# Window attention and two feed-forward layers on one core: the written list of the first pass is laid out anew

## Chip, core and metric

The kernel runs on one core of a Trainium2 chip. The metric is the device time of one execution in microseconds (us). The core has a matrix engine (TensorE, PE in the profile; its weight loads are PEld), three elementwise engines (VectorE is DVE, ScalarE is ACT, GpSimd is POOL) and a queue that starts transfers (SyncE, SP). Each engine takes its instructions strictly in the order in which the program hands them over, and waits where an operand or a buffer is not ready.

## The reference

```python
k_sum = k.reshape(B, H, nb, block, D).max(axis=3)      # B,H,S,D = 2,8,768,64; block 32
v_sum = v.reshape(B, H, nb, block, D).mean(axis=3)
scores_l = where(|i - j| < 16, q @ k.T / sqrt(D), -1e9)
scores_s = q @ k_sum.T / sqrt(D) + log(block)
a = softmax(concat([scores_l, scores_s]))
x = (a @ concat([v, v_sum])).transpose(0, 2, 1, 3).reshape(1536, 512)
h = relu(x @ w_in1); x = (h * h) @ w_out1               # 512 -> 2048 -> 512
h = x @ w_in2; P = a0 + a1*h + a2*h^2 + a3*h^3
out = (P / (1 + |b0|*|h| + |b1|*h^2 + 1e-6)) @ w_out2
```

## The kernel before

Attention is cut into 12 **units** (256 tokens by 4 heads), each of two **duos**, 24 in all. The feed-forward layers keep each operand as a coarse part and a remainder (`wh`, `wl`, `xh`, `xl`, `sh`, `sl`) and make three matmuls for a product. They run in four passes over the weights. The first pass takes only the first 5 of the 16 column blocks of layer 1, token group after token group (four of 256 tokens, one of 512), so 25 steps, and it runs while attention is still under way. From there on a loop (`main_loop`) orders the work; until there the order is a list written out by hand, `ORDER`, of 783 items. A program walks through it and emits each item's instructions, so the list alone fixes what stands behind what on every engine. An item is a letter and a number; a `*` means that a copy is made by VectorE where it would otherwise be made by ScalarE or GpSimd.

- Transfers (SP): `E F` keys, `q_ Q` queries, `v Z` and `N` values, `J` keys of the second batch, `I` raw weights (three buffers).
- Keys and block sums: `P R` rearranging copies, `t` transposes on PE, `l k` copies out of PSUM, `c B` block maxima; `S` sums on GpSimd, `V` matmuls, `u w` copies.
- Attention of unit u: `q` transposes, `z` copy. Of duo d: `s` scores (PE, matrix `pss`; both duos of a unit must be done before either goes on), `m` mask and row maximum (VectorE, L505), `e` exponentials (ScalarE, L514), `r` row sum and reciprocal (VectorE, L522, L523), `n` normalising (GpSimd, L529), `p` transposes (PE, `ptp`), `b` copy (`pp`, ScalarE or VectorE), `o` the product with values (PE, `pav`). Then `x` coarse part (ScalarE) and `y` remainder (VectorE) of the unit's output.
- Weights, half a block each: `T` (ScalarE, L146), `D` (VectorE, L154 and L155), `W` (ScalarE, L166), `M` (GpSimd, L171). Tile `wdec` has two buffers, so `T` of n waits for `M` of n-2.
- First pass: `h` a quarter of a step of layer 1 (three matmuls, L612), `i` relu (ScalarE, L622), `j` square (VectorE, L627), `G` coarse part (ScalarE, L675), `H` remainder (GpSimd, L682), `Y` a quarter of a step of layer 2 (three matmuls, L706). Steps 0 to 3, 4 and so on are `h0` to `h3`, ...; the last five steps (`h80` to `h99`) take 512 tokens at once and need the last four units. `X` are filling matmuls with no use but to keep PE busy.

Six PSUM banks go round among `pk`, `pt`, `pss`, `ptp`, `pvs`, `pav`: a bank is reused in the order in which the list gives it back. The walk through the list:

```python
for x in ORDER.split():
    ...
    elif x[-1] == "*":
        parts[x[0]](int(x[1:-1]), dve)
    else:
        parts[x[0]](int(x[1:]))
main_loop()
```

Of the kernel before, what the change touches and what calls it, by code (L numbers as in the profile page):

```python
# [16 lines left out]


ORDER = (
    "E0 _i0 X8 _m0 _id _m1 F0 K0 P0 F1 E1 E2 q_0 F2 _bw I0 E3 q_1 R0* P1 F3 t0 X2 _ml R1 t1 l0 "  # L20
    "P2 k0 q0 _m2 l1 k1 R2 z0 v0 c0 P3 X3 t2 c1 v1 l2* R3 s0 s1 q1 Q1 S0 _pr k2 T0 I1 v3 B0 t3 "
    "c2 m0 B1 S1 D0 B2 e0 z1 m1 N0 l3* e1 r0 r1 n0 k3 V0 W0 p0 q2 v2 u0 c3 z2 n1 w0 s2 s3 m2 e2 "
    "r2 T1 b0* M0 m3 N1 n2 B3* D1 p1 I2 S2 s4 s5 m4 q3 p2 e3 S3 N2 N3 b1* e4 o0 o1 r3 I3 n3 V1 "
    "z3 m5 T2 x0 p3 r4 u1 W1 D2 w1 n4 M1 b2* W2 b3* e5 y0 h0 M2 o2 o3 x1 p4 s6 s7 m6 r5 T3 h1 I4 "
    "y1 h2 O0 h3 e6 T4 D3 i0 D4 n5 Q2 h4 h5 j0 W3 b4 h6 p5 q4 W4 M3 m7 q5 M4 h7 z4 i1 G0 I5 H0 "
    "h8 e7 r6 h9 I6 N4 Y0 b5* Y1 Y2 Y3 h10 j1 T5 r7 n6 N5 T6 z5 D5 h11 p6 J1 D6 o4 o5 n7 W5 i2 "
    "G1 J0 s8 s9 m8 M5 W6 b6* I7 p7 m9 x2 b7 M6 t4 e8 H1 j2 I8 y2 T7 T8 h12 h13 N6 h14 N7 l4* "
    "_b8 D7 Y4 D8 J2 h15 Y5 J3 Y6 Y7 i3 N9 W7 G2 W8 H2 o6 o7 M8 Y8 x3 Y9 Y10 Y11 M7 e9 j3 I9 h16 "
    "h17 r8 r9 h18 h19 k4 n8 y3 h20 i4 h21 j4 G3 H3 n9 T9 h22 N11 h23 Z0 h24 Y12 Y13 D9 Y14 J5 "
    "Y15 I10 h25 h26 i5 j5 h27 h28 N8 h29 p8 G4 W9 H4 M9 t5 i6 G5 Y16 Y17 H5 Y18 Y19 h30 Y20 j6 "  # L30
    "b8 I11 N10 Y21 Y22 h31 Y23 I12 i7 S4 p9 h32 G6 h33 l5 s10 s11 m10 e10 r10 n10 h34 j7 h35 "
    "b9* h36 Q3 Q4 H6 m11 e11 o8 o9 p10 Y24 r11 Y25 Y26 T10 D10 Y27 n11 i8 h37 T11 G7 b10* I13 "
    "h38 k5* j8 h39 p11 W10 x4 H7 i9 Y28 Y29 G8 D11 H8 Y30 Y31 Y32 y4 b11 W11 c4 Y33 Y34 J4 o10 "
    "o11 M10 V2 J6 J7 M11 x5 h40 h41 y5 T12 h42 h43 i10 j9 G9 Y35 t6 Z1 D12 W12 h44 H9 Y36 c5 "
    "T13 k6* q6 z6 j10 h45 D13 Y37 h46 M12 h47 Y38 i11 G10 H10 Y39 h48 B4 l6 Y40 Y41 Y42 I14 u2 "
    "N13 j11 Y43 B5* h49 h50 N15 h51 i12 h52 t7 W13 c6 G11 w2 h53 l7* h54 S5 H11 h55 k7 j12 s12 "
    "s13 m12 e12 r12 Y44 m13 Y45 n12 i13 G12 c7 T14 H12 I15 Y46 Y47 q7 e13 r13 p12 Y48 M13 Y49 "
    "Y50 q8 z7 b12 Y51 s14 s15 N12 n13 j13 z8 h56 D14 m14 h57 m15 p13 h58 e14 h59 b13 r14 B7 N14 "
    "i14 V3 I16 n14 G13 e15 o12 o13 u3* H13 Q5 w3* p14 T15 Y52 r15 Y53 Y54 Y55 x6 y6 W14 h60 b14 "
    "n15 p15 j14 q9 b15* h61 D15 B6 o14 o15 M14 x7 s16 s17 m16 e16 y7 h62 h63 h64 W15 M15 m17 "  # L40
    "h65 h66 z9 i15 G14 I17 H14 Y56 e17 Y57 Y58 j15 r16 h67 i16 G15 n16 r17 Y59 h68 T16 h69 h70 "
    "H15 h71 Y60 j16 i17 Y61 G16 I18 Y62 H16 N18 n17 Y63 T17 D16 j17 Y64 N17 Y65 Y66 h72 Y67 N16 "
    "W16 N19 h73 q10 D17 p16 s18 s19 m18 e18 r18 z10 I19 h74 M16 h75 m19 b16* h76 p17 n18 W17 "
    "e19 i18 G17 b17* o16 o17 M17 I20 H17 j18 r19 s20 s21 m20 N21 p18 x8 Y68 m21 e20 N20 Y69 Y70 "
    "n19 Y71 r20 e21 n20 h77 b18* y8 h78 q11 h79 z11 p20 r21 p19 s22 s23 m23 b19* n21 o18 o19 "
    "i19 m22 G18 e23 p21 H18 N22 Y72 r23 e22 b21* b20 r22 Y73 n23 x9 n22 T18 Y74 o20 o21 x10 y9 "
    "T19 p23 b23* y10 N23 Y75 p22 h80 b22 j19 o22 o23 h81 D18 I21 x11 W18 y11 h82 h83 i20 M18 "
    "D19 G19 h84 h85 H19 h86 j20 T20 Y76 Y77 W19 Y78 h87 Y79 h88 i21 M19 h89 j21 G20 h90 H20 h91 "
    "D20 Y80 i22 Y81 G21 Y82 I22 H21 Y83 T21 D21 Y84 W20 Y85 M20 Y86 Y87 T22 h92 h93 j22 h94 W21 "
    "h95 i23 I23 h96 h97 M21 G22 h98 H22 D22 h99 Y88 j23 Y89 Y90 W22 Y91 i24 G23 j24 H23 M22 T23 "  # L50
    "D23 W23 M23 "
)


# [854 lines left out]
```

## Time and profile before

| | |
|---|---|
| time before, median of 3 runs | 633.11 us (631.19 to 633.25) |
| the profiled execution's own time | 633.35 us |
| its span, first to last instruction | 631.6 us |
| PE busy over the span | 601.4 us (95%) |
| DVE, ACT, POOL busy | 380.6, 389.6, 347.8 us (60%, 62%, 55%) |
| mean clock granted to PE | 0.981 |

The profiled execution is 0.24 us above the median. Nearly 2 us lie outside the span. In the second half of the span PE stands at nine tenths or more in every slice, so read the first ten of the 40 slices of the page for anything that another order of the list can touch.

### The profile page before, as it was taken

How to read it: one execution, taken by the hardware profiler on the slowest of the kernel's cores; microseconds unless marked ns; L12 is line 12 of the kernel's file. 1: busy time of each engine (PE TensorE's matmuls, PEld its weight loads, DVE VectorE, ACT ScalarE, POOL GpSimd, SP SyncE). 2: the span in 40 equal slices, each digit the busy share in tenths (PEclk: the TensorE clock that was granted, in tenths of full speed). 3: DMA queues.
4: the chain of work that ended last, by engine and by line, in shares of the span. 5: the costliest groups of instructions: out<-in, count | busy, mean ns of one | idle time of the engine just before them, and what ended most of it. 6: DMA issues, size and time to landing. Idle time of an engine off the chain costs nothing.

```text
span 631.6 us, 9882 instructions
## 1 busy us (share of the span) xinstructions
PE 601.4 (95%) x3578; PEld 506.5 (80%) x3578; DVE 380.6 (60%) x791; ACT 389.6 (62%) x715; POOL 347.8 (55%) x363
## 2 busy tenths in 40 slices
PE   6678999888999999999999999999999999999997
PEld 6568887777888888888888888888888888888885
DVE  5776387757644333111146477898787887676775
ACT  5566456745544444222156678989888988777772
POOL 3667767553464444422277658776655774444442
PEclk8788999989999999999999999999999999999999
DMA  9949967421333323000024410221201300010011
GB/s 219 240 130 216 231 158 179 118 79 42 116 108 100 100 81 97 1 0 1 0 68 168 134 33 34 67 67 35 66 34 33 101 1 1 1 66 1 10 58 66
DMA packets 65376, 51.49 MB, mean 82 GB/s; under 512 B 39856, under 2 KB 59056, under 8 KB 65328
## 3 DMA queue, kind: packets, MB, share of 16 engines
q1 hardware_dynamic: 65184, 50.74, 29.4%
q8 instruction: 28, 0.46, 0.3%
q14 instruction: 20, 0.16, 0.1%
q10 hardware_dynamic: 144, 0.13, 0.1%
HBM read 47.71 MB, written 3.15 MB: 81 GB/s over the span
## 4 chain that ended last, share of the span: by engine, by line
PE 86%; DVE 5%; POOL 2%; DMA 2%; ACT 2%; issue 1%; SPq 0%; DVEq 0%; POOLq 0%; ACTq 0%
PE h L612 40%; PE y L706 40%; DMA early<-in_k_dram 2%; PE pav L559 2%; PE pss L489 2%; DVE pr L505 1%; ACT pr L514 1%; POOL pr L529 1%; PE ptp L539 1%; DVE mx L522 1%; DVE pp L543 1%; POOL sl L682 1%; PE pk L402 1%; PE pvs L441 1%; PE pt L467 0%
## 5 line engine op out<-in xcount | busy, mean ns | idle before, releaser
L612 PE MATMUL h<-xl,wh 128*128 128x512 f32 (+1 forms) x424 | 157.5, 371 | 5.0 <-DVE xl L581 3.7
L612 PE MATMUL h<-xh,wh 128*128 128x512 f32 (+1 forms) x424 | 158.7, 374 | 2.0 <-DVE r L627 2.0
L612 PE MATMUL h<-xh,wl 128*128 128x512 f32 (+1 forms) x424 | 156.9, 370 | 0.7 <-POOL wl L171 0.7
L682 POOL TENSOR_TENSOR sl<-r,sh 128x512 fp32r<-128x512 f32 (+1 forms) x58 | 65.5, 1129 | 105.8 <-PE y L706 76.0
L636 POOL TENSOR_TENSOR q<-q,u 128x512 f32<-128x512 f32 x48 | 65.2, 1359 | 96.1 <-ACT q L633 94.2
L627 DVE TENSOR_TENSOR r<-r,h 128x512 f32<-128x512 f32 (+1 forms) x58 | 34.3, 592 | 117.0 <-ACT r L622 107.3
L612 PEld LDWEIGHTS h<-xl,wh 128*128 128x128 f32 x424 | 80.3, 189 | 19.5 <-DVE xl L581 6.3
L612 PEld LDWEIGHTS h<-xh,wh 128*128 128x128 f32 x424 | 80.3, 189 | 16.6 <-DVE r L627 2.2
L171 POOL TENSOR_TENSOR wl<-wdec,wh 128x512 fp32r<-128x512 f32 x64 | 83.4, 1309 | 17.4 <-ACT wh L166 13.0
L612 PEld LDWEIGHTS h<-xh,wl 128*128 128x128 f32 x424 | 80.2, 189 | 14.2 <-POOL wl L171 0.9
L706 PE MATMUL y<-sl,wh 128*128 128x512 f32 (+1 forms) x232 | 82.7, 357 | 1.3 <-POOL sl L682 0.8
L706 PE MATMUL y<-sh,wh 128*128 128x512 f32 (+1 forms) x232 | 83.0, 358 | 0.0
L706 PE MATMUL y<-sh,wl 128*128 128x512 f32 (+1 forms) x232 | 82.0, 353 | 0.0
L622 ACT ACTIVATE r<-h 128x512 f32<-128x512 f32 (+1 forms) x58 | 30.3, 522 | 81.3 <-PE h L612 43.1
L706 PE MATMUL y<-wh,sl 128*128 128x512 f32 x192 | 74.9, 390 | 0.1
L706 PE MATMUL y<-wh,sh 128*128 128x512 f32 x192 | 74.7, 389 | 0.0
L706 PE MATMUL y<-wl,sh 128*128 128x512 f32 x192 | 74.7, 389 | 0.0
L682 POOL TENSOR_TENSOR sl<-p,sh 128x512 fp32r<-128x512 f32 x48 | 63.1, 1316 | 8.5 <-ACT sh L675 7.2
L658 DVE SCALAR_TENSOR_TENSOR q<-q,h 128x512 f32<-128x512 f32 x48 | 32.9, 686 | 41.6 <-ACT h L654 41.6
L529 POOL TENSOR_SCALAR pr<-pr,rs 128x120 f32<-128x120 f32 x96 | 38.8, 425 | 31.1 <-DVE rs L523 20.4
L706 PEld LDWEIGHTS y<-sl,wh 128*128 128x128 f32 x232 | 44.0, 190 | 8.8 <-POOL sl L682 2.8
L166 ACT CAST wh<-wdec 128x512 fp32r<-128x512 f32 x64 | 39.7, 620 | 18.1 <-DVE wdec L155 17.1
(92 smaller groups left out, 1055.6 us busy)
## 6 DMA issues: line engine op xcount, KB each, us to landing
wraw<-in_moe_w_in_dram SPq DMA_DIRECT2D x32, 512.0 KB, 3.9
wraw<-in_moe_w_out_dram SPq DMA_DIRECT2D x32, 512.0 KB, 3.3
early<-in_v_dram SPq DMA_DIRECT2D x40, 96.0 KB, 4.8
out_dram<-acc SPq DMA_DIRECT2D x11, 256.0 KB, 2.1
acc<-in_q_dram SPq DMA_DIRECT2D x10, 256.0 KB, 5.8
early<-in_k_dram SPq DMA_DIRECT2D x8, 192.0 KB, 4.8
early<-in_v_dram SPq DMA_DIRECT2D x4, 384.0 KB, 7.2
kst<-in_k_dram SPq DMA_DIRECT2D x8, 192.0 KB, 4.2
```

Source lines behind the costliest of these rows:

```text
L166: nc.scalar.copy(out=wt[n][0][:, j], in_=f32(wdec[n, j]))
L171: nc.gpsimd.tensor_tensor(out=tl[:, j], in0=t, in1=f32(th[:, j]), op=ALU.subtract)
L489: nc.tensor.matmul(psc[u][e][w * LO:(w + 1) * LO, c * HK:(c + 1) * HK], lhsT=qz[u % 2][r, c * P + w * LO:c * P + (w + 1) * LO], rhs=kt[2 * ...
L529: nc.gpsimd.tensor_scalar(out=pr[:, c, 0:HK], in0=pr[:, c, 0:HK], scalar1=rs[:, c:c + 1], scalar2=1.0, op0=ALU.mult, op1=ALU.mult,)
L559: nc.tensor.matmul(pav[u][e * D:(e + 1) * D, c * P + w * LO:c * P + (w + 1) * LO], lhsT=vn[u % 2][j][:, w, f:f + D], rhs=po[2 * u + e][:, ...
L612: nc.tensor.matmul(hq[g][:, 0:n], lhsT=w[:, 0, ws], rhs=x[:, part, ts], start=(part == 0 and j == 0), stop=(part == KC - 1 and j == 2),)
L622: nc.scalar.activation(out=r, in_=hq[g][:, 0:n], func=AF.Relu)
L627: nc.vector.tensor_tensor(out=eq[g], in0=eq[g], in1=hq.pop(g)[:, 0:n], op=ALU.mult)
L636: nc.gpsimd.tensor_tensor(out=q_, in0=q_, in1=u_, op=ALU.mult)
L658: nc.vector.scalar_tensor_tensor(out=q_, in0=q_, scalar=1.0 + 1e-6, in1=z_, op0=ALU.add, op1=ALU.mult)
L682: nc.gpsimd.tensor_tensor(out=sl[:, 0:n], in0=eq.pop(g), in1=f32(sh[:, 0:n]), op=ALU.subtract)
L706: nc.tensor.matmul(o, lhsT=lt, rhs=rt, start=(f == 0 and j == 0 and d * m % 512 == 0), stop=(f == FS[ps] - 1 and j == 2 and (d + 1) * m % ...
```

## The change

Only the string `ORDER` differs. It has the same 783 items, but the 783 stand in another order, and 24 copies have another engine. From ScalarE or GpSimd to VectorE go `P0 k0 R1 R2 w1 k7 b12 u2 w2 b14 b20 b22`, from VectorE to ScalarE or GpSimd `R0 l2 b1 b2 b5 b6 l4 l7 B5 b16 b21 b23`. Nothing is computed otherwise. Two stretches of the table, around `s18`:

```diff
-    "W16 N19 h73 q10 D17 p16 s18 s19 m18 e18 r18 z10 I19 h74 M16 h75 m19 b16* h76 p17 n18 W17 "
-    "e19 i18 G17 b17* o16 o17 M17 I20 H17 j18 r19 s20 s21 m20 N21 p18 x8 Y68 m21 e20 N20 Y69 Y70 "
...
+    "q11 G12 H12 Y46 Y47 s18 s19 W11 z11 m18 r17 N15 o14 e18 o15 h56 h57 h58 Y48 G13 h59 Y49 N17 "
+    "p16 m19 Y50 Y51 i14 N16 n17 r18 b16 p17 H13 h60 s20 s21 b17* o16 x7 o17 N19 n18 M11 h61 y7 "
+    "h62 j14 h63 h64 h65 e19 m20 r19 n19 e20 G14 H14 r20 n20 p18 b18* x8 N18 Y52 Y53 Y54 Y55 p19 "
```

ScalarE near the start, from the second and third block sums (`early<-pvs`) to the first coarse output of attention (`xh<-pav`), of before:

```order
L474 COPY qz_86<-pt 128x512
L146 ACTIVATE wdec<-wraw 128x512
L576 CAST xh<-pav 128x2x256
L449 COPY early<-pvs 24x256 x2
L166 CAST wh<-wdec 128x512
```

and of the change:

```order
L448 COPY early<-pvs 24x256 x4
L542 COPY pp_89<-ptp 120x512
L448 COPY early<-pvs 24x256 x2
L513 ACTIVATE pr_102<-pr_102,mx_90 128x120 x4
L473 COPY qz_85<-pt 128x512
L145 ACTIVATE wdec<-wraw 128x512
L473 COPY qz_86<-pt 128x512
L575 CAST xh<-pav 128x2x256
```

The first output now stands behind the block sums of both units, one more group of exponentials and both copies of queries of units 4 and 5; PE makes the scores of duos 6 and 7 and the transposes of 3, 4 and 5 ahead of the first product.

PE around the transposes of duo 17 (`ptp<-ident,pr_104`), of before (the names behind `pav` are the copies of duos 16 and 17):

```order
L612 MATMUL h<-xl,wh 128x256
L612 MATMUL h<-xh,wl 128x256
L539 MATMUL ptp<-ident,pr_104 120x128 x4
L559 MATMUL pav<-pp_88,early 64x64
L559 MATMUL pav<-pp_89,early 64x64
```

and of the change:

```order
L705 MATMUL y_1580<-sl,wh 128x256
L538 MATMUL ptp<-ident,pr_104 120x128 x4
L611 MATMUL h<-xh,wh 128x256
L611 MATMUL h<-xl,wh 128x256
L611 MATMUL h<-xh,wl 128x256
L488 MATMUL pss<-kt_98,qz_85 64x120 x8
L488 MATMUL pss<-kt_99,qz_85 64x120 x8
L558 MATMUL pav<-pp_88,early 64x64
```

Between the transposes and the product that needs their copy there now stand a quarter step of layer 1 and the scores of the next unit.

VectorE in the last steps of the pass, from the last remainder of attention (`xl<-pav,xh`), of before:

```order
L581 TENSOR_TENSOR xl<-pav,xh 128x2x256
L154 TENSOR_SCALAR wdec<-wdec 128x512
L155 SCALAR_TENSOR_TENSOR wdec<-wraw,wdec 128x512
L627 TENSOR_TENSOR r<-r,h 128x512
L718 COPY acc<-y_1848 128x512
L627 TENSOR_TENSOR r<-r,h 128x512
L154 TENSOR_SCALAR wdec<-wdec 128x512
```

and of the change:

```order
L580 TENSOR_TENSOR xl<-pav,xh 128x2x256 x3
L626 TENSOR_TENSOR r<-r,h 128x256
L153 TENSOR_SCALAR wdec<-wdec 128x512
L154 SCALAR_TENSOR_TENSOR wdec<-wraw,wdec 128x512
L153 TENSOR_SCALAR wdec<-wdec 128x512
L154 SCALAR_TENSOR_TENSOR wdec<-wraw,wdec 128x512
L626 TENSOR_TENSOR r<-r,h 128x512
L153 TENSOR_SCALAR wdec<-wdec 128x512
```

Two weight conversions stand ahead of the first square of the last five steps where one stood; from `h80` on the list has 11 conversions `D` where it had 6.

## Rows read from the trace of the kernel before

**Rows 1.** The page: busy time of PE, and its granted clock by slice.
```profile
PE 601.4 (95%) x3578; PEld 506.5 (80%) x3578; DVE 380.6 (60%) x791; ACT 389.6 (62%) x715; POOL 347.8 (55%) x363
...
PEclk8788999989999999999999999999999999999999
```

**Rows 2.** Busy time of each engine in four stretches of the first pass.
```profile
core 0: us, PE busy (x) PEld busy (x) DVE busy (x) ACT busy (x) POOL busy (x), PEclk, DMA share, GB/s
0.00:63.27 63.27, 47.25 (x518) 41.84 (x519) 42.51 (x166) 39.06 (x95) 38.12 (x69) 0.87 0.87 201
63.27:130.54 67.27, 61.62 (x672) 56.47 (x670) 45.99 (x147) 41.51 (x106) 44.38 (x72) 1.00 0.70 164
130.54:155.14 24.60, 20.69 (x286) 18.76 (x284) 14.81 (x70) 13.32 (x37) 13.18 (x31) 0.86 0.26 69
155.14:181.13 25.99, 25.40 (x144) 20.55 (x142) 14.82 (x21) 12.16 (x23) 11.68 (x10) 1.00 0.32 102
```

**Rows 3.** Timeline of PE: start, duration, instructions; transposes, products and scores of attention.
```profile
50.27 0.60 PE L539 MATMUL ptp<-ident,pr 128*120 128x128 f32 x4
50.80 1.15 PE L559 MATMUL pav<-pp,early 120*64 120x64 f32 x32
51.88 1.05 PE L489 MATMUL pss<-kt,qz 64*64 64x120 f32 x32
```

**Rows 4.** Timeline of PE: quarter steps of 256 tokens, and the last of 512.
```profile
63.27 0.28 PE L612 MATMUL h<-xh,wh 128*128 128x256 f32 x1
...
63.63 0.28 PE L612 MATMUL h<-xh,wh 128*128 128x256 f32 x1
...
180.28 0.39 PE L706 MATMUL y<-sh,wh 128*128 128x512 f32 x1
...
180.97 0.39 PE L612 MATMUL h<-xh,wh 128*128 128x512 f32 x1
```

**Rows 5.** Timeline, one unit's chain; in brackets idle time and its releaser.
```profile
75.70 1.05 PE L489 MATMUL pss<-kt,qz 64*64 64x120 f32 x32
...
78.42 0.66 DVE L522 TENSOR_REDUCE mx<-pr 128x4 f32<-128x484 f32 x1 [0.71 <-ACT pr L514]
79.46 1.39 POOL L529 TENSOR_SCALAR pr<-pr,rs 128x120 f32<-128x120 f32 x4 [3.60 <-DVE rs L523]
```

**Rows 6.** Timeline, from the transposes of duo 17 to its product.
```profile
134.74 0.62 PE L539 MATMUL ptp<-ident,pr 128*120 128x128 f32 x4
136.95 1.28 DVE L543 COPY pp<-ptp 120x512 f32<-120x512 f32 x2
137.74 2.52 PE L559 MATMUL pav<-pp,early 120*64 120x64 f32 x32 [2.38 <-ACT pr L514]
```

**Rows 7.** Timeline, near the start: filling matmuls, and a weight conversion.
```profile
1.12 3.47 PE L290 MATMUL spare<-pp 120*128 120x128 f32 x16 [1.12 <-DVE pp L284]
...
26.57 1.21 DVE L154 TENSOR_SCALAR wdec<-wdec 128x512 int32<-128x512 int32 x1
27.82 1.36 DVE L155 SCALAR_TENSOR_TENSOR wdec<-wraw,wdec 128x512 int32<-128x512 int32 x1
```

**Rows 8.** Timeline, weight conversions of the last steps on four engines.
```profile
156.16 0.42 DVE L154 TENSOR_SCALAR wdec<-wdec 128x512 int32<-128x512 int32 x1
156.61 0.69 DVE L155 SCALAR_TENSOR_TENSOR wdec<-wraw,wdec 128x512 int32<-128x512 int32 x1
159.02 1.29 POOL L171 TENSOR_TENSOR wl<-wdec,wh 128x512 fp32r<-128x512 f32 x1 [4.10 <-ACT wh L166]
159.06 1.54 DVE L154 TENSOR_SCALAR wdec<-wdec 128x512 int32<-128x512 int32 x1
161.51 0.68 ACT L146 ACTIVATE wdec<-wraw 128x512 f32<-128x512 f32 x1
163.90 0.62 ACT L166 CAST wh<-wdec 128x512 fp32r<-128x512 f32 x1
183.69 1.29 POOL L171 TENSOR_TENSOR wl<-wdec,wh 128x512 fp32r<-128x512 f32 x1 [1.28 <-ACT wh L166]
```

58 rows, old and new, of the table ORDER are left out of this document.

## The prediction

> **What bounds the kernel now.** Read the page first. PE is busy for 601.4 of 631.6 us, and its granted clock is short of full only in the first ten slices [rows 1]. So the kernel is a PE program, and what the list can change is the time that PE loses before `main_loop` takes over. Next cut the first pass into stretches and ask of each how much PE work at full clock lies in it. A quarter step of 256 tokens is followed by the next after 0.36 us, one of 512 after 0.69 us [rows 4]. A duo costs 0.53 us of transposes, half of 1.08 us of products and some 0.46 us of scores [rows 3]. The pass has 160 quarter steps of 256 tokens (57.6 us) and 32 of 512 (some 21.8 us at 0.68), 24 duos (36.6 us), and I put some 19 us to queries, keys, block sums and filling matmuls: about 135 us. Its last `Y` ends at 181.1 us [rows 2, 4], so 46 us are lost. Walking along the list with these prices, the PE work ahead of `h16` is 36.9 us and it starts at 63.27 us; ahead of `h72` it is 93.8 (130.54 us); ahead of `h80` 110.9 (155.14 us). So **stretch A** up to `h16` loses 26.4 us, **stretch B** from `h16` to `h80` takes 91.87 us for 74.0 us of work and loses 17.9 (10.4 up to 130.54, then 7.5), and **stretch C** from `h80` to the end of the last `Y` takes 25.99 for 24.3 and loses 1.7 [rows 2].
>
> In B no other engine is full: DVE is busy for 60.8 of 91.9 us, ACT for 54.8, POOL for 57.6 [rows 2]. Its loss is waiting, and the rows show for what. The scores of a unit end at 76.75 us; mask, exponentials, row sum and normalising follow one another until 80.85 us [rows 5], so a unit's first duo comes back to PE no sooner than **4.1 us** after its scores. PE must have other work queued for so long. At the end of the pass it has not: behind duo 17's transposes, done at 135.36 us, comes the product that needs their copy, which stands behind DVE's next masks and starts only at 136.95 us as one of two copies; PE starts on the product at 137.74 after 2.38 us idle and then takes 2.52 us for it [rows 6], where the same 32 instructions took 1.15 us before [rows 3]: the granted clock of this stretch is 0.86 [rows 2], that is, part of it ran at 1.2 GHz. An empty queue is thus paid twice.
>
> **The change, part by part.** No instruction is added or removed, so the PE work stays at 135 us. The sum is over the three stretches, with the same markers, since the work ahead of `h80` is 110.9 us in both lists and that behind it 24.3.
>
> *Stretch B.* I counted, in both lists, the PE work queued between the end of a unit's scores and the first transposes that need them. Before, units 5, 6, 7, 9, 10 and 11 have 2.1, 1.8, 3.5, 3.6, 3.5 and 3.7 us: all under the 4.1 us of the chain. Units 4 and 8 have 13.1 and 9.0. In the new list units 4 to 11 have 12.7, 25.7, 8.3, 10.8, 12.0, 9.1, 6.5 and 7.7 us. For unit 9 this is the stretch shown in the diff: before, three quarter steps, one set of transposes, two duos' products and two of scores (3 x 0.36 + 0.53 + 1.08 + 0.91 = 3.6); now two more of products, eleven quarter steps more and another set of transposes (9.1). From the last transposes to the product it was 0 to 2.7 us in these units and is now 1.1 to 9.2; the copy itself needs some 0.7 us (half of 1.28 [rows 6]). So every place where this stretch waits for a unit's chain has more cover than the chain is long. The cover comes from doing attention earlier: `o17` stood behind 98.9 us of PE work and now behind 88.7. What is left over are waits that I still find by following the queues with row durations: the transposes of the sixth key pair wait for a copy on ACT (some 1.2 us), `q9` for its queries, whose transfer is queued behind values that wait for `o9` (0 to 1.7), `Y32` for `H8` on POOL (0 to 1), duo 17's transposes for a normalising step behind two weight conversions (0.8). That is 2 to 5 us; I take **5**, the upper end, as such a walk sees no handing over between engines. 73.3 + 5 = 78.3 us against 91.9. Bounds: nothing left over (73.3), and all of the 17.9 (91.2).
>
> *Stretch A.* `h16` now stands behind 37.6 us of PE work instead of 36.9, and the work on DVE, ACT and POOL ahead of it is the same within 1.2 us. No engine has less to do; only the waits differ. Two things are worse. The 16 filling matmuls, which began at 1.12 us and took 0.217 us each [rows 7] where a transpose of the same 128 columns later takes 0.13 [rows 3], now stand behind the first transposes, which so run at the lower clock too: about +1 us. And attention is pushed ahead: `o0` stands behind 19.9 us of PE work instead of 14.1, `h0` behind 22.4 instead of 18.1. Better is that products come 8.7 and 4.8 us of PE work after the transposes of units 0 and 1, where it was 1.9 and 0.4. I followed the new queues by hand, each step with the mean duration of its kind. Scores of duo 0 come at 11.6 us (the filling matmuls hold PE until 9.5; then transposes, two key copies and the copy of queries). Those of duo 2 come at 20.2, since the copy of their queries now stands behind two groups of exponentials, a key copy and two weight steps. Those of duo 4 at 25. The block sums come at 28.7, as their sums on POOL stand behind two normalisings and a weight step. `o0` comes at 37, behind both block sums (5 us of PE) and the transposes of duos 3, 4 and 5, each of which waits for POOL. `h0` follows at 40.5, `Y0` at 48.6 and `h16` at 57.5, as the scores up to duo 11 are made by then and PE has mostly first-pass steps queued. That has each conversion `D` at its undisturbed 1.1 us [rows 8]; while POOL worked, one took 2.6 [rows 7]. Nine `D` and the POOL steps that they hold up lie ahead of `h16`; at 0.5 us each that gives **62.0**, against 63.27. Bounds: 57.5, and 67.3 if the 4.3 us by which `h0` moves back in PE work are all paid.
>
> *Stretch C.* Six conversions become eleven. Their busy time fits: 11 x 1.11 us on DVE, 11 x 1.30 on ACT, 12 x 1.29 on POOL [rows 8], under 16 us each beside 24.3 of PE. What could be late is `j`, `G`, `H` behind them. The chain of one weight is 0.68 + 1.11 + 0.62 + 1.29 = 3.7 us, two at a time, so some 2 us each: from `h80` on the last `M` would come at 27 to 30 us, and the first `H` behind it is needed at 32.4 (24.3, and then three blocks of four quarter steps at 2.7 each, which `main_loop` puts ahead of it). I take 24.3 + 2.3 = **26.6**, and 24.3 and 31 as bounds.
>
> A conversion's first step takes 0.42 us alone and 1.54 us when POOL's remainder started just ahead of it, and it ends with it [rows 8]. The Trainium skill, "SBUF — State Buffer", section "SBUF: two separate sides", says that VectorE's two-port operations and GpSimd share a pair of ports that one of them holds for a whole instruction. By that rule all eleven could wait so, 11 x 1.1 = 12 us more on DVE; the trace agrees as to the row, and the sum above goes without it.
>
> *Sum.* 62.0 + 78.3 + 26.6 = 166.9 us against 181.1: 14.2 us less. Behind the pass nothing changes: PE is busy for the whole of it, and all 24 weight halves are ready in both lists. 633.35 - 14.2 = 619.1 for the profiled execution, which stands 0.24 above the median: **619 us**.
>
> **The rivals.** *Waits handed on.* The chain is covered, but engines that run closer behind one another lose by small waits what they gain: B keeps 11 us of its loss (84.3), A gains nothing (63.3), C takes 27.6. Together 175.2, 5.9 less: some 627 us. For it: DVE and ACT work ahead of `h40` is 8 us more than before. Against: they are busy for two thirds of B at most [rows 2].
>
> *All of it comes back.* A at 58, B at 75 and C at 25.5 give 158.5, 22.6 less: 610 us. Against it: the row of 2.6 us for one conversion is one of before's A, and the new list has nine there as well.
>
> *The same waits elsewhere.* B's and A's changes cancel: 633 us. The 24 copies that change engine alone would do nothing else. Against it speaks the cover counted above.
>
> *Slower: the weight train of C.* In the rows before, six conversions took from 156.16 to 184.98 us [rows 8], 4.8 us each. If that were their pace and not the list's, eleven take 53 us, the first `H` behind them is ready at 54 instead of 32.4, and PE is 22 us late: 619 + 22 = 641. From 4.1 us a weight on it takes the whole gain (11 x 4.1 + 1.3 - 32.4 = 14.0). Against it: before, they were listed one behind each `h` step, and chains with two buffers need half of it.
>
> **How the numbers follow.** A measurement of this kernel can tell about 0.3% (1.9 us) from no change. Chances: the forecast, 614 to 624 us, 0.48; handed on, 624 to 631.2, 0.22; all back, under 614, 0.10; the same waits, 631.2 to 635, 0.08; slower, 0.12. The range from 611 to 633 leaves out 0.04 below and 0.16 above. Faster 0.80, same 0.08, slower 0.12.
>
> **What would show it.** Right: `h80` starts near 140 us, no gap of over 1 us on PE between 62 us and there, the granted clock full in it, `h16` near 62, the last `Y` of the pass done near 167. Wrong for A: `h0` later than 46 us. Wrong for B: gaps in front of `ptp` or `pav` still there, or moved to `h` and `y` with POOL or ACT as releaser. Wrong for C: PE waits for `sl` or `wl` after `h80`.

## The result and the profile after

| | before | after |
|---|---|---|
| median of 4 runs | 632.35 us (631.19 to 633.25) | 617.87 us (617.46 to 618.33) |
| the profiled execution's own time, span | 633.35, 631.6 us | 617.69, 616.0 us |
| mean granted clock | 0.981 | 0.994 |

The ratio is 0.977, with a 95% interval of 0.975 to 0.979. The forecast was 619, so its number is right within 0.2%. Its parts are not: the first pass is shorter than forecast by 6.9 us, and behind it 5.4 us are lost where nothing was to change.

The page of the changed kernel, busy time of PE and its granted clock in 40 slices, against [rows 1]:

```profile
PE 590.7 (96%) x3578; PEld 500.0 (81%) x3578; DVE 386.9 (63%) x794; ACT 389.9 (63%) x714; POOL 347.3 (56%) x361
...
PEclk9799999999999999999999999999999999999999
```

One slice of 40 stands below 9 where five did. The windows of the changed kernel with the same markers as [rows 2] (up to `h16`, to `h80`, to the end of the last `Y`, and 26 us behind the pass):

```profile
core 0: us, PE busy (x) PEld busy (x) DVE busy (x) ACT busy (x) POOL busy (x), PEclk, DMA share, GB/s
0.00:59.89 59.89, 44.70 (x547) 39.34 (x547) 43.56 (x184) 41.12 (x101) 39.08 (x72) 0.94 0.84 204
59.89:135.51 75.62, 74.14 (x951) 71.19 (x948) 55.27 (x192) 46.94 (x124) 48.17 (x91) 1.00 0.60 140
135.51:160.03 24.52, 24.52 (x119) 20.36 (x117) 14.63 (x21) 13.36 (x24) 15.64 (x12) 1.00 0.44 138
160.03:186.00 25.97, 21.41 (x93) 17.04 (x92) 18.10 (x23) 15.05 (x27) 15.88 (x12) 1.00 0.48 149
```

Stretch A fell from 63.27 to 59.89 us, B from 91.87 to 75.62, C from 25.99 to 24.52: 21.1 us less. B now has PE busy for 74.1 of 75.6 us at full clock. The last row is new: PE has 21.4 us of work in 26. In the kernel before, the 26 us behind the pass were full:

```profile
181.13:207.10 25.97, 25.97 (x116) 21.49 (x116) 11.12 (x18) 12.69 (x23) 14.13 (x11) 1.00 0.32 102
```

What stands there shows in the waits of PE in the changed kernel, from 60 us to the end (total, times, longest):

```profile
PE h L611 <- DVE r L626: 2.8, 1, 2.8
PE pk L401 <- DVE pk L392: 1.5, 2, 1.1
PE y L705 <- POOL sl L681: 1.3, 1, 1.3
PE y L705 <- ACT sh L674: 0.5, 1, 0.5
```

The second of them lies in B (the sixth key pair). The other three start at 160.0, 172.5 and 171.3 us, behind the pass; they sum to 4.6 of the 5.4 us lost there, and the rest does not show as waits. The waits of PE in the kernel before, from 63 us to the end of the pass, were:

```profile
PE pav L559 <- ACT pr L514: 2.4, 1, 2.4
PE h L612 <- DVE r L627: 2.0, 1, 2.0
PE h L612 <- DVE xl L581: 1.9, 3, 1.3
PE pav L559 <- issue: 1.2, 1, 1.2
PE ptp L539 <- POOL pr L529: 1.1, 1, 1.1
PE y L706 <- POOL sl L682: 0.8, 2, 0.5
PE pav L559 <- DVE pp L543: 0.3, 1, 0.3
```

None of them is left in B. At the place of [rows 6], duo 17, the timeline of the changed kernel reads:

```profile
110.73 0.60 PE L538 MATMUL ptp<-ident,pr 128*120 128x128 f32 x4
...
111.62 1.05 PE L488 MATMUL pss<-kt,qz 64*64 64x120 f32 x32
112.60 1.15 PE L558 MATMUL pav<-pp,early 120*64 120x64 f32 x32
```

No idle time stands ahead of the product, and its 32 instructions take 1.15 us again instead of 2.52.

Now the first wait behind the pass. ScalarE, VectorE and GpSimd in the changed kernel:

```profile
157.08 2.73 POOL L170 TENSOR_TENSOR wl<-wdec,wh 128x512 fp32r<-128x512 f32 x2 [1.28 <-ACT wh L165]
...
158.59 0.67 ACT L145 ACTIVATE wdec<-wraw 128x512 f32<-128x512 f32 x1 [0.53 <-POOL wl L170]
160.91 0.62 ACT L165 CAST wh<-wdec 128x512 fp32r<-128x512 f32 x1 [1.64 <-DVE wdec L154]
161.43 0.59 ACT L621 ACTIVATE r<-h 128x512 f32<-128x512 f32 x1
...
162.05 0.69 DVE L626 TENSOR_TENSOR r<-r,h 128x512 f32<-128x512 f32 x1 [1.24 <-ACT r L621]
...
162.80 0.50 PE L611 MATMUL h<-xh,wh 128*128 128x512 f32 x1 [2.77 <-DVE r L626]
```

Read it backwards. PE's first quarter step behind the pass (162.80) needs the PSUM bank that `j23` (162.05) gives back. `j23` waits for `i23` on ScalarE (161.43). The quarter steps `h92` to `h95` that `i23` reads had been done at 154.6 us, but `i23` stands behind `W20` (160.91), which waits for the conversion `D20`, which waits for `T20` (158.59), which had waited for its buffer from GpSimd's `M18` (157.08). A step that was ready 7 us earlier stands in line behind a weight that PE needs much later.

### The profile page after: what moved, and what is told of

Same layout as the page of the kernel before. It is cut to its first block, busy times and chain, and to the rows that moved or that the text cites. A ratio compares the mean times of both kernels' runs of the same rounds, so it can differ in the third digit from the quotient of the medians.

```text
span 616.0 us, 9880 instructions
## 1 busy us (share of the span) xinstructions
PE 590.7 (96%) x3578; PEld 500.0 (81%) x3578; DVE 386.9 (63%) x794; ACT 389.9 (63%) x714; POOL 347.3 (56%) x361
## 4 chain that ended last, share of the span: by engine, by line
PE 69%; DVE 3%; ACT 2%; issue 1%; POOL 0%; DVEq 0%; ACTq 0%; POOLq 0%
PE h L611 35%; PE y L705 35%; DVE wdec L154 1%; DVE wdec L153 1%; ACT wdec L145 1%; ACT r L621 0%; DVE acc L737 0%; POOL wl L170 0%; DVE r L626 0%; DVE h L660 0%; DVE q L657 0%; ACT wh L165 0%; ACT sh L674 0%; ACT h L653 0%; DVE p L663 0%
## 5 line engine op out<-in xcount | busy, mean ns | idle before, releaser
L170 POOL TENSOR_TENSOR wl<-wdec,wh 128x512 fp32r<-128x512 f32 x64 | 84.3, 1323 | 14.7 <-ACT wh L165 14.5
L154 DVE SCALAR_TENSOR_TENSOR wdec<-wraw,wdec 128x512 int32<-128x512 int32 x64 | 56.3, 879 | 2.2
```

The lines of the kernel that those rows point to most:

```text
L154: nc.vector.scalar_tensor_tensor(out=t, in0=low, scalar=29, in1=t, op0=ALU.logical_shift_right, op1=ALU.bitwise_or)
L170: nc.gpsimd.tensor_tensor(out=tl[:, j], in0=t, in1=f32(th[:, j]), op=ALU.subtract)
```

## The experiments

No list leaves out any work. The times by stretch come from one profiled execution each, with the markers used above; "behind" is its own time less the end of the last `Y`.

| | median us | ratio to before | A | B | C | behind |
|---|---|---|---|---|---|---|
| before | 632.35 | | 63.27 | 91.87 | 25.99 | 452.22 |
| after | 617.87 | 0.977 (0.975 to 0.979) | 59.89 | 75.62 | 24.52 | 457.66 |
| E1 engines back | 626.10 | 0.989 (0.986 to 0.992) | 59.19 | 83.07 | 24.52 | 457.70 |
| E2 engines alone | 632.60 | 1.000 (0.999 to 1.002) | 63.60 | 91.55 | 25.53 | 452.20 |
| E10 two copies back | 623.39 | 0.986 (0.983 to 0.988) | 59.64 | 81.02 | 24.52 | 457.68 |
| E4 no cover | 632.12 | 1.000 (0.998 to 1.001) | 59.26 | 90.66 | 24.51 | 457.66 |
| E12 last unit uncovered | 626.04 | 0.990 (0.989 to 0.992) | 60.45 | 82.84 | 24.51 | 457.75 |
| E8 cover in before's list | 629.05 | 0.995 (0.993 to 0.997) | 63.52 | 87.33 | 25.99 | 452.20 |
| E6 steps ahead | 619.28 | 0.979 (0.976 to 0.982) | 59.24 | 75.98 | 24.52 | 459.54 |
| E3 conversions spread | 619.69 | 0.980 (0.978 to 0.982) | 60.18 | 80.62 | 24.50 | 454.38 |
| E13 third buffer | 616.95 | 0.977 (0.975 to 0.979) | 60.04 | 75.62 | 24.55 | 456.74 |
| E14 remainder on VectorE | 615.26 | 0.972 (0.970 to 0.975) | 60.26 | 75.62 | 24.52 | 454.99 |
| E5 filling first | 616.30 | 0.975 (0.972 to 0.977) | 58.03 | 75.61 | 24.52 | 457.76 |
| E9 cover and tail | 613.47 | 0.970 (0.968 to 0.972) | 59.62 | 76.16 | 24.52 | 453.49 |

The last column carries much of the argument: it is 457.66 to 457.76 in every list that ends as the changed one does, whatever happens ahead, and 452.20 to 452.22 in the three that end as before. The 5.4 us belong to the last lines of the list and to nothing else.

### E1, E2 and E10: the engines of the 24 copies

E1 is the new order with before's engines, E2 the old order with the new engines, E10 the new order and engines with `k7` and `l7` alone exchanged again. The edits have this form (E10; in stretches of the list, here and below, `...` stands for what is left out):

```diff
-    "... Y23 k7* Y24 c7 ..."
+    "... Y23 k7 Y24 c7 ..."
...
-    "... t7 l7 N9 ..."
+    "... t7 l7* N9 ..."
```

> The changed list in its new order, but the 24 copies on the engines of before. Theory (the order of the list, and with it the cover of each unit's chain, gives the gain): 616 to 621 us, the gain stays. Rival (the copies that change engine carry a good part of it): 623 us or more.

> The list of before in its old order, with the 24 copies on the engines of the change. Theory (order gives the gain): 630 to 637 us, nothing gained. Rival (the engines carry a good part): 627 us or less.

> The changed list with only k7 back on ScalarE and l7 back on VectorE. Theory (with all 24 copies back 8 us were lost, most of it because k7 on ScalarE stands behind e13 and b11, so that c6 and c7 and the scores of unit 7 are late): 4 to 6 us more than the change, 622 to 624 us. Rival (the loss is spread over many copies): within 2 us of the change, 617 to 620 us.

E2 came out at no change, as expected. E1 did not: without the engines the new order loses 8.2 of the 14.5 us, nearly all in B (83.07 against 75.62). A owes nothing to the engines (59.19). In E1's B the waits of PE for the scores sum to 5.1 us, and the granted clock stood at 0.54 from 86.5 to 90.0 us. E10 loses 5.5 us by two copies, within what was expected. The rows of E1 at the place, VectorE and PE:

```profile
82.77 0.95 DVE L421 TENSOR_REDUCE kss<-kt 128x24 f32<-128x768 f32 x1 [4.32 <-ACT kt L413]
...
85.49 1.14 PE L488 MATMUL pss<-kt,qz 64*64 64x120 f32 x32 [3.42 <-DVE kt L427]
```

and ScalarE in E1 ahead of them:

```profile
80.23 0.34 ACT L427 COPY kt<-kss 128x192 f32<-128x192 f32 x1
80.47 1.25 ACT L513 ACTIVATE pr<-pr,mx 128x120 f32<-128x120 f32 x4
81.63 0.57 ACT L542 COPY pp<-ptp 120x512 f32<-120x512 f32 x1
82.09 0.64 ACT L413 COPY kt<-pk 128x576 f32<-128x576 f32 x1
```

In the changed kernel `k7` runs on VectorE and the block maxima follow at once:

```profile
77.42 0.75 DVE L413 COPY kt<-pk 128x576 f32<-128x576 f32 x1
78.28 0.95 DVE L421 TENSOR_REDUCE kss<-kt 128x24 f32<-128x768 f32 x1
```

On ScalarE, in E1, it stands behind a block-maxima copy, a group of exponentials and another duo's copy, and comes 4.7 us later; VectorE idles for 4.3 us, and PE for 3.4 at the scores of unit 7. The order moved attention so far forward that the key copies became the step next in line, and the engine of a copy then decides.

### E4, E12 and E8: the cover

E4 puts all quarter steps and their copies that stand between `s18` and `o23` behind `o23`; E12 does it only between `s22` and `o23` (23 quarter steps, 8.3 us). E8 goes the other way: before's list, with six quarter steps moved behind `s19`, where PE had 3.6 us of cover.

```diff
-    "... s18 s19 W11 z11 m18 r17 N15 o14 e18 o15 h56 h57 h58 Y48 G13 h59 Y49 N17 p16 m19 Y50 Y51 i14 ..."
+    "... s18 s19 W11 z11 m18 r17 N15 o14 e18 o15 N17 p16 m19 ..."
...
+    "... b22* o22 o23 h56 h57 h58 Y48 G13 h59 Y49 Y50 Y51 i14 ..."
```

> The changed list, but all first-pass items (h, i, j, G, H, Y) that stand between s18 and o23 are put behind o23, in their order. The same work, attention as early as before or earlier, but the last units have some 4, 2 and 2 us of PE work between scores and transposes. Theory (cover decides): PE waits in front of ptp and pav for units 9 to 11 and its clock falls; 8 to 14 us are lost, 626 to 632 us. Rival (it is enough that attention is done earlier and the other engines are ahead): within 2 us of the change, 616 to 620 us.

> After's list with only the 23 quarter steps between s22 and o23 (8.3 us of PE work) put behind o23, that is, the cover of the last units alone is taken away. Cover theory: PE waits for up to two chains of 4.1 us there, part of it at the lower clock, so 4 to 8 us are lost: 622 to 626 us, h80 4 to 8 us later, o23 earlier. Rival (E4's 14 us came from the order of attention as a whole, not unit by unit): 617 to 619 us.

> The list of before with six quarter steps (Y64 Y65 Y66 h72 Y67 h73), which stood just ahead of the scores of unit 9, put just behind them. Theory (cover decides; unit 9 then has 5.8 us instead of 3.6 between scores and transposes): the 2.4 us wait ahead of its product shrinks and the clock stays up; 2 to 5 us less than before, 627.5 to 630.5 us. Rival (cover taken from in front of the scores is only moved): 631.5 to 634 us.

E4 gives the whole gain back: B is 90.66 us. E12 loses 7.2 us of B for the cover of the last two units alone. Both end at the upper edge of what was expected, 0.1 us above it in E4 and 0.04 in E12, so the missing cover cost as much as was thought possible. E8 gains 3.1 us, against 632.15 us of the list of before in the same group of runs, with nothing but six quarter steps in another place. The 2.4 us wait of [rows 6] shrinks to two of 0.2 and 0.3, and the granted clock from 130.5 to 150.9 us is 1.00, where it was 0.86 [rows 2]. The waits of PE in E12 around the last units:

```profile
PE pav L558 <- ACT pp L542: 1.1, 1, 1.1
PE ptp L538 <- POOL pr L528: 1.0, 1, 1.0
PE pav L558 <- issue: 0.8, 1, 0.8
PE pav L558 <- DVE xl L580: 0.6, 1, 0.6
```

These are waits of the kind that the list of before had, back in the changed list. They sum to 3.5 us, and B is 7.2 longer. Two more groups of transposes take 1.31 and 1.34 us instead of 0.60, while GpSimd's four normalising steps for them (1.39 us) are still running, which is some 1.4 us more; and another part is the clock. E12's windows, from `s22` on:

```profile
121.44:132.54 11.10, 7.30 (x128) 5.11 (x129) 5.76 (x25) 5.61 (x15) 3.74 (x10) 1.00 0.34 84
132.54:135.95 3.41, 3.41 (x32) 3.29 (x28) 0.00 (x0) 0.11 (x1) 0.73 (x1) 0.50 0.01 2
```

PE was busy for 7.3 of 11.1 us, and then the granted clock stood at 0.50, the lower level (1.2 GHz), for 3.4 us in which it had work all the time; half of that, 1.7 us, is lost. E4 shows it larger: after a stretch of waits the granted clock was 0.50 from 122.9 to 133.1 us, and from 104 to 115 us it was 0.84 on the mean. E4's `o23` ends at 130.5 us, earlier than the 135.1 of the changed kernel: attention as such was faster, and the time was lost all the same.

### E6, E3, E13 and E14: the loss behind the pass

E6 lists `i23 j23 G23 H23` ahead of `W19` and the same of step 24 ahead of `T22` (the second move, and the start of the loop, which then leaves out `G24 H24`, are not shown below). E3 spreads the conversions from 13 on over the last units and the last steps. E13 keeps the list and gives conversions 14, 17, 20 and 23 a third scratch tile. E14 keeps the list and makes the remainder of conversions 14 to 23 on VectorE.

```diff
-    "... h96 h97 M18 W19 T20 h98 D20 M19 I23 W20 Y88 M20 i23 j23 T21 D21 G23 H23 T22 ..."
+    "... h96 h97 M18 i23 j23 G23 H23 W19 T20 h98 D20 M19 I23 W20 Y88 M20 T21 ..."
```

```diff
+        if 2 * n + j in (14, 17, 20, 23):
+            t = qz[0].bitcast(I32)
+        else:
             t = hp.tile([P, DM], I32, tag="wdec", name="wdec")
```

```diff
-        nc.gpsimd.tensor_tensor(out=tl[:, j], in0=t, in1=f32(th[:, j]), op=ALU.subtract)
+        eng = nc.vector if 14 <= 2 * n + j < 24 else nc.gpsimd
+        eng.tensor_tensor(out=tl[:, j], in0=t, in1=f32(th[:, j]), op=ALU.subtract)
```

> The changed list, but at its end i23 j23 G23 H23 are put ahead of W19, and i24 j24 together with G24 H24 (which the loop would otherwise emit) ahead of T22; the last conversions stand behind them. Theory (PE loses 5.4 us right behind the pass because relu and square of steps 23 and 24 stand behind a weight conversion that waits for a buffer): 4 to 5.5 us less, 612.5 to 614 us. Rival (the conversions' own throughput is the bound and the wait only moves to later steps): 616.5 to 618.5 us.

> The changed list with conversions 13 to 16 put in among the last units (from o19 on, where DVE, ACT and POOL are busy for a half to two thirds) and 17 to 23 spread evenly behind h80; nothing else moves. Theory (eleven conversions at 2.9 us each in the last 25 us are too many, whatever their order; they cost 5.4 us behind the pass): 4 to 5.5 us less than the change, 612.5 to 614 us. Rival (the conversions get in the way of the last units' chains, which wait instead): 616 to 620 us.

> After's list, word for word; only the scratch tile of the conversions 14, 17, 20 and 23 is another one (a tile that attention no longer needs), so that the train has three buffers instead of two. Theory (the pace of 2.9 us per half is that of a chain of 3.7 us and more in two buffers, where the first step of n waits for the last of n-2): the pace falls to some 2.4 us, the last conversion ends near 167 instead of 172.5, the waits behind the pass fall from 7 to 3 us or less: 613 to 615.5 us. Rival (the pace is that of the order on each engine, and of POOL and VectorE holding each other up): 617 to 618.5 us, and the last conversion within 1.5 us of where it was.

> After's list, word for word; only the last step (remainder) of the conversions 14 to 23 is made by VectorE instead of GpSimd, in the same place of the list. In the changed kernel the two VectorE steps of a conversion take 1.63 us on the mean from h80 on where they take 1.11 undisturbed. Theory (what slows the train, since it was not the two buffers, is VectorE's steps running longer while GpSimd works beside them): these steps fall to 1.2 us, a conversion's chain gets shorter by 0.5 us there and by some 0.6 at the remainder (0.69 instead of 1.29), the last conversion ends before 168 us instead of 172.5, and the waits behind the pass fall from 4.6 to 2 us or less: 613.5 to 616 us. Rival (the order of the list on each engine sets the pace, or VectorE now lacks what GpSimd gave): the last conversion within 1.5 us of where it was, or later, 617 to 620 us.

E6 missed. The three waits went, and one larger came, on PE in E6:

```profile
177.98 0.79 PE L705 MATMUL y<-sh,wh 128*128 128x512 f32 x1 [4.64 <-ACT acc L727]
```

Steps 23 and 24 were early, so the next thing needed from ScalarE was the eviction of a finished `y`, which `main_loop` puts behind the whole list and so behind the conversions pushed back. The granted clock was 0.50 from 175.87 to 182.69 us. The loss behind the pass grew to 7.3 us.

E3 brought it down to 2.2 us and paid 5.0 in B, as its rival had it. The longest single wait: a remainder on GpSimd (130.91 us) now stands ahead of a normalising step of the last units, whose transposes then wait 1.0 us and take 1.35 instead of 0.60; two waits for `sl` in B make 1.0 more, and what makes the rest stays open.

E13 missed too: the last conversion ends at 171.87 us instead of 172.51, and the 0.9 us gained lie within the intervals. Two buffers are not what sets the pace. The waits of PE behind the pass did fall, from 4.6 to 2.4 us, as was expected, but the clock took most of that back (see the last section).

E14 gained 2.6 us. VectorE's two steps of a conversion from `h80` to 173 us, in the changed kernel (instructions, busy time, mean ns of one, idle time before):

```profile
L154 DVE SCALAR_TENSOR_TENSOR wdec<-wraw,wdec 128x512 int32<-128x512 int32 x11 | 10.5, 956 | 0.4
L153 DVE TENSOR_SCALAR wdec<-wdec 128x512 int32<-128x512 int32 x12 | 8.1, 674 | 8.7 <-ACT wdec L145 8.6
```

and in E14:

```profile
L154 DVE SCALAR_TENSOR_TENSOR wdec<-wraw,wdec 128x512 int32<-128x512 int32 x12 | 8.3, 692 | 0.4
L153 DVE TENSOR_SCALAR wdec<-wdec 128x512 int32<-128x512 int32 x12 | 7.0, 580 | 6.6 <-ACT wdec L145 6.6
```

They fall from 1.63 to 1.27 us, the last conversion ends at 170.0 us, and the waits of PE behind the pass fall from 4.6 to 1.9 us. The time lies in the range of the theory; the last conversion comes earlier by about half of what it said. So VectorE's steps were slowed while GpSimd worked beside them. How much of the 2.6 us comes from that is not shown: E14 also makes the remainder itself shorter (0.69 us instead of 1.29) and frees GpSimd for `H`. That most of the rest of the pace is the order of the list on each engine is likely, but no run shows it by itself.

### E5 and E9: the start, and all together

E5 lists the 16 filling matmuls first again, as before. E9 does this as well, places conversions 12 to 15 where an engine idles in the last units, and lists each of the last steps ahead of the conversions.

```diff
-    "_m0 E0 K0 _pr _bw _id P0* _i0 F0 E1 _b8 R0 t0 l0 F2 k0* X8 ..."
+    "_i0 X8 _m0 E0 K0 _pr _bw _id P0* F0 E1 _b8 R0 t0 l0 F2 k0* ..."
```

> The changed list with the filling matmuls and the memset that they need put first, as before. Theory (their late place costs the start about 1 us, but the scores of duo 2 wait for the copy of queries behind two weight steps anyway): h0 comes up to 1 us earlier, 616.8 to 618 us. Rival (the lower clock at the start is passed on through the whole first stretch): 615.5 us or less.

> After's list with the filling matmuls first (as E5), conversions 12 to 15 put in places between the last two units where no duo's copy or normalising step follows them on their engine, and, in the last five steps, each step's relu, square, coarse part and remainder listed ahead of the conversions. Theory (behind the pass only the train of conversions is late, and it is late because it starts late and stands ahead of the steps' own copies): the loss behind the pass, 5.4 us in the changed kernel, goes, and the pass itself stays: 616.3 - 5 = 611 to 613 us. Rival (the train takes on some engine what PE then lacks, wherever it stands, as E3 showed): 615 to 618 us, h80 later by 2 us or more.

E5 gained 1.6 us, which lies between the spans of its theory and its rival, and its interval overlaps that of the changed kernel. E9 gained 4.4: it is the fastest of all, 0.970 of before, though just above its expected span. B is 0.5 longer than in the changed kernel, and the loss behind the pass falls from 5.4 to 1.3 us. Its waits of PE from 60 us on:

```profile
PE pk L401 <- DVE pk L392: 1.5, 2, 1.1
PE y L705 <- POOL sl L681: 0.8, 1, 0.8
```

So the train of conversions takes little from PE if it starts early in idle places and stands behind the steps. E9 does both at once; which of the two does more is not shown.

## Why the prediction was right, and where it was not

Of what was to show it, `h16` came at 59.9 us instead of near 62, `h80` at 135.5 instead of near 140, the last `Y` ended at 160.0 instead of near 167, and `h0` began at 42.7, before 46. Between `h16` and `h80` one gap of over 1 us is left (1.09 at 72.08 us), and the clock is full. The sign for C, PE waiting for `sl`, appeared, but behind the pass.

**Stretch B** was right in its mechanism. E4, E12 and E8 move nothing but first-pass steps with their copies, and the time moves as the count of cover says, in E4 and E12 down to the lower clock behind the waits. The term was mis-sized: 75.62 instead of 78.3. Of the 5 us of small waits that it added, 1.5 show as waits, at the transposes of the sixth key pair and the next one. There PE waited for the zeroing of the bank on VectorE, which ran at 71.95 us behind the masks of unit 6, and not for a copy on ScalarE. The waits of `q9`, `Y32` and duo 17 did not come.

**Stretch A** gained 3.4 us, not 1.3. The hand walk gave 57.5 and was 2.4 us short; the 4.5 us added for nine slowed conversions were too much. Those nine took 12.0 us on VectorE (835 and 495 ns a step) against 10.0 at the undisturbed price, so 0.2 us each and not 0.5. That is close to the 2.4, but A was not tried by itself, and what sets it stays open. That it owes nothing to the engines, E1 shows. "About +1 us" for the filling matmuls: E5 gained 1.6, not clear of noise. The reason given, that the first transposes run at the lower clock, is not what the rows show: the granted clock is 1.00 up to 4.6 us in the kernel before and up to 11.3 us in the changed one, although eight transposes took 1.49 us there and 0.85 at 15.85 us.

**Stretch C** fell to 24.52, the bare work, not to 26.6: within the pass the train held nothing up.

**The step that failed** is "Behind the pass nothing changes". Its reason was that PE is busy throughout and that all 24 weight halves are ready. The halves were ready; what was late were the pass's own last steps, which stand among the conversions on ScalarE. The prediction did price the train, but at 2 us a half where the changed kernel takes 3.2 (`M13` and `M23` end at 140.97 and 172.51), and it looked only at the first `H` behind the last conversion. That the PSUM bank of the first `h` behind the pass hangs on an `i` inside the train was not followed. E9 and E6 show that the place decides: with the same conversions and steps in another order the loss is 1.3 us in E9 and 7.3 in E6. The rival of the slower train had the cause right and not the place: it put the loss of the whole gain at 4.1 us a half, and 5.4 us were lost at 3.2. The Trainium skill, "SBUF — State Buffer", section "SBUF: two separate sides", has VectorE's two-port operations and GpSimd exclude one another. E14 agrees with it as to the direction (1.63 to 1.27 us a conversion); by the estimate from that rule the eleven conversions would take 12 us more on VectorE, and they took 5.7 (0.52 each). In [rows 8] VectorE's step ended 0.3 us behind GpSimd's (160.60 against 160.31 us), and not with it.

**The copies.** "The 24 copies that change engine alone would do nothing else" is true of the old list (E2) and misleads: in the new one they are worth 8.2 us (E1), two of them 5.5 (E10). The sum held, since it was made for both together.

So 619 is the sum of two errors that nearly cancel: 6.9 us too long for the pass, 5.4 too short behind it. That the number came within 0.2% is luck: with nothing lost behind the pass the kernel would have taken some 612 us (an estimate, 617.7 less 5.4).

## What to carry to other kernels

Where engines take work strictly in order, count the work queued on the bound engine between the start of a dependent chain and the first use of its result, and compare it with the chain's length; an uncovered chain was paid here in waiting and, in E4 and E12, again at the lower clock. Moving work that is not urgent forward or back is free only if no step that is urgent stands behind it on any of the engines that it uses, so for the end of a rearranged stretch ask which buffer the next stage needs first, and what stands ahead of the instruction that gives it back. An edit that does nothing alone (E2) can carry half the gain (E1) together with another, so test it in both settings.

## What was not expected

The pace of PE at the start differs from one execution to another. E5 and E9 begin with the same instructions of PE, and the same eight transposes start at 4.70 us in both. The timeline of E5:

```profile
4.70 0.89 PE L401 MATMUL pk<-ident,early 96*128 96x96 f32 x8
7.41 0.85 PE L401 MATMUL pk<-ident,early 96*128 96x96 f32 x8 [1.82 <-DVE pk L392]
```

and of E9:

```profile
4.70 1.49 PE L401 MATMUL pk<-ident,early 96*128 96x96 f32 x8
8.42 1.51 PE L401 MATMUL pk<-ident,early 96*128 96x96 f32 x8 [2.23 <-DVE pk L392]
```

The granted clock in the windows of both is 1.00 there (up to 8.2 us in E5, up to 14.1 in E9), so it does not account for the difference, whose cause stays open. `h0` comes at 40.79 us in E5 and at 42.38 in E9, and the lists are the same up to there. So 1.6 us of A hang on the execution, as much as E5 gained, and only the times of several runs (615.38 to 617.03 against 617.46 to 618.33) speak for that edit.

A wait is not followed by a low clock each time. After the 2.77 us of the changed kernel at 160 us the granted clock stayed at 1.00; in E13, after 1.9 us at the same place, its windows read

```profile
160.21:162.96 2.75, 0.81 (x3) 0.67 (x4) 1.52 (x3) 2.52 (x5) 1.36 (x2) 1.00 0.72 239
162.96:166.38 3.42, 3.42 (x10) 2.65 (x9) 3.23 (x3) 0.94 (x3) 2.84 (x2) 0.50 0.52 144
```

that is, 3.42 us at the lower level (1.2 GHz), of which 1.7 are lost, so that E13's own gain is hidden in part. Of the price of a wait the profile shows one case, not the mean.
